# A delta-rule attention with a feed-forward part on one core: pieces placed by a time in us, a third place for converted weights, all low parts on TensorE

## The chip, the cores and the metric

One NeuronCore of a Trainium2 chip. The metric is the device time of one execution in microseconds (us). The core has five engines with a queue each: TensorE (PE; its weight loads are shown as PEld), VectorE (DVE), ScalarE (ACT), GpSimd (POOL) and SyncE (SP), which here only issues DMAs. An engine runs its instructions in the order in which they were written down for it; waits are semaphores.

## What is computed

```python
# q, k, v: (4, 8, 768, 48); beta: (4, 8, 768); w_in: (384, 2048); w_out: (2048, 384)
k_n = k / (norm(k) + 1e-6)
for t in range(S):                                   # per batch and head
    y[t] = q[t] @ state                              # state: 48 x 48
    state = state + beta[t] * outer(k_n[t], v[t] - state.T @ k_n[t])
x = y, heads side by side                            # (3072, 384)
h = x @ w_in
out = (h * tanh(softplus(h))) @ w_out                # (3072, 384)
```

The two weight matrices come as float64 numbers. The kernel reads them as pairs of 32-bit integers and makes of each number a high and a low part.

## The kernel before

**Chunks and units.** The sequence is cut into 12 chunks (`NS`) of 64 steps, for all 32 heads together. Chunk n gives 256 rows of x, and `moe(n)` runs the feed-forward part on them: this is unit n. A unit has eight pieces `fp`; `g1(fp)` is 18 matmuls of `h` (L528) and behind them a chain `e` over ScalarE and VectorE (L532 to L550) that ends in `g`, high and low part; `g2(fp)` is 12 matmuls into `acc` (L562), two pieces later. The low part of `g` is made by GpSimd in units 0 to 2 (`pg=3`) and by VectorE afterwards.

**Chunks, two at a time.** `early(g)` makes for chunks 2g and 2g+1 the products of the keys (`pg`), scales them (`ss`, `y`, `rc`, `nb`) and inverts a triangular matrix step by step on VectorE (`pr`, `gt`, L294 and L299), ending in transposes (`tt`, `tu`, `tn`). For g = 0 and 1 the inverse is made in two halves (28 steps), and `merge(n)` joins them with two matmul stages (`ma`, `mb`). Then come, per chunk, the stages `s_a`, `s_b` (`ta`, `tb`), and per half of the heads `s_gq`, `s_z`, `s_y` (`gq`, `pz`, `py` and `ps`), each followed by copies out of PSUM. `turn(n)` transposes the 256 rows `yy` (`xt`) and splits them into a high and a low `x`, with which unit n can start.

**Weights.** 28 pieces, 12 of `w_in` (names `ri`, `mi`, `wi`, 512 columns) and 16 of `w_out` (`ro`, `mo`, `wo`, 384 columns). `convert` (L177 to L204) turns one into a value `a` by one ScalarE and four VectorE operations, writes the high part rounded to float32r by ScalarE (L195), and for the first 22 pieces (`pl=22`) has TensorE add `a` and the high part through an identity in float32 (L199, L200; PSUM tile `lo`) and ScalarE write the low part (L201). The last six low parts are made by VectorE (L203). `a` has two places (tag `w`).

**The order.** `plan` holds generators with a time each, in units of a feed-forward pass from a table `TN`; they are advanced in the order of the times, and each writes down the whole of a piece at once, with the operations behind a matmul stage included. The instructions then go through a list scheduler that may move them on each engine within their dependencies and its own forecast of time. Two things bind it: `queue` chains instructions of VectorE in the written order (conversions, the first inverses, some of the stages of chunk 0), and from the time `m0=-0.05` on TensorE's order is as written. `keep_warm` writes filler matmuls on zeros behind chosen instructions (`warm`, L583).

Of the kernel before, what the change touches and what calls it, by code (L numbers as in the profile page):

```python
# [34 lines left out]
def kernel(  # L35
# [32 lines left out]
    P = 128  # L68
# [22 lines left out]
    nc.scalar.preload_act_table_set("natural_log_exp_and_others")  # L91

# [69 lines left out]
    chain = []  # L162

    def queue(ins, on=True):

        if not on:
            return
        if chain:
            order(ins, chain[-1])
        chain.append(ins)  # L170

# [4 lines left out]

    def convert(kind, i):  # L177
        st = raw[kind, i].rearrange("p (a b) -> p a b", b=2)
# [6 lines left out]
        nc.scalar.activation(a, high.bitcast(F32), AF.Abs, scale=2.0 ** -80)  # L185
        queue(nc.vector.tensor_scalar(a, a, F64_LEAST * 2.0 ** -80, F64_MOST * 2.0 ** -80, op0=ALU.max, op1=ALU.min))
        yield
        queue(nc.vector.tensor_scalar(ai, ai, 3, None, op0=ALU.logical_shift_left))
        yield
        queue(nc.vector.scalar_tensor_tensor(ai, high, 0x7FFFFFFF, ai, op0=ALU.bitwise_or, op1=ALU.bitwise_and))  # L190
        yield
        queue(nc.vector.scalar_tensor_tensor(ai, st[:, :, 0], 29, ai, op0=ALU.logical_shift_right, op1=ALU.bitwise_or))
# [3 lines left out]
        if parts.index((kind, i)) < TN['pl']:  # L196

            ps = pa.tile([P, 512], F32, tag="at", name=f"lo{kind}{i}")[:, :n]
            nc.tensor.matmul(ps, ident, a, start=True, stop=False)  # L199
            nc.tensor.matmul(ps, ident, w[:, 0].bitcast(F32), start=False, stop=True)  # L200
            nc.scalar.mul(out=w[:, 1], in_=ps, mul=-1.0)  # L201
        else:
            queue(nc.vector.scalar_tensor_tensor(w[:, 1], a, -1.0, w[:, 0], op0=ALU.mult, op1=ALU.subtract))  # L203
        yield  # L204
# [4 lines left out]
    def early(g):  # L209
# [3 lines left out]
        for t2 in range(2):  # L213
# [7 lines left out]
            queue(m, g < QK and g < 2)  # L221
            if g > 1:
                if TN.get('kp', 1):
                    tc.keep_in_program_order(m)
# [4 lines left out]
            for h8 in range(2):  # L229
                ps = pa.tile([P, 8, C], F32, tag="at", name=f"pg{n}_{h8}")  # L230
                for p8 in range(8):
                    p = 8 * h8 + p8

                    for c in range(2):
                        for hh in range(2):
# [22 lines left out]
        queue(nc.vector.tensor_scalar(ss, gf[:, ::33], 1e-30, None, op0=ALU.max), qg)  # L258
# [18 lines left out]
        queue(nc.vector.tensor_tensor(  # L277
            out=blk, in0=blk, in1=nb.rearrange("p (x j) -> p x j", x=nb_).unsqueeze(2).broadcast_to(by_col),
            op=ALU.mult), qg)
        nc.gpsimd.memset(gf[:, ::33], 1.0)  # L280
        bp = ap.tile([P, 32], F32, tag="bp", name=f"bp{g}")
        queue(nc.vector.tensor_scalar(bp, nb, -1.0, None, op0=ALU.mult), qg)
        ne = nes[g] = ap.tile([P, 32], F32, tag="ne", name=f"ne{g}")
        queue(nc.vector.transpose(ne, ss), qg)  # L284
        yield
        for j in range(1, sz - 1):
# [5 lines left out]
            eng = nc.gpsimd if g in TN.get('ps', ()) and TN.get('j0', 0) <= j < TN.get('j1', 31) else nc.vector  # L292
            on = qg and eng is nc.vector
            queue(eng.tensor_tensor(out=pv, in0=nj, in1=xj, op=ALU.mult), on)  # L294
            if g == 0 and j == TN.get('jt', 7):
                x = nc.tensor.matmul(warm[:, :64], zero[:, 0:P], pr[:, 0:64], start=True, stop=True)  # L296
                keep_warm(4 * TN.get('wt', 24), x)
            yield
            queue(eng.tensor_tensor(out=below, in0=below, in1=pv, op=ALU.add), on)  # L299
            yield  # L300
        queue(nc.vector.tensor_tensor(
            out=blk, in0=blk, in1=bp.rearrange("p (x i) -> p x i", x=nb_).unsqueeze(3).broadcast_to(by_col),
            op=ALU.mult), qg)
        if not split:
            yield
        queue(nc.vector.transpose(tt2[:, :, :, 32:].rearrange("p a b i -> p i (a b)"), gt), qg)
        tn = tns[g] = ap.tile([P, 2, NP, 32], F32, tag="tn", name=f"tn{g}", bufs=1)
        if split:
            tu = tus[g] = ap.tile([P, 2, NP, 16], F32, tag="prod", name=f"tu{g}", bufs=1)
            queue(nc.vector.transpose(tu.rearrange("p a b j -> p j (a b)"),  # L310
                                      gt[:, :, 0:16].rearrange("p i j -> p j i")), qg)
            ym = yms[g] = ap.tile([P, 33, 32], F32, tag="gt", name=f"ym{g}", bufs=1)
            nc.gpsimd.memset(ym[:, :32, 16:], 0.0)
        else:
            queue(nc.vector.transpose(tn.rearrange("p a b j -> p j (a b)"), gt.rearrange("p i j -> p j i")), qg)
# [9 lines left out]
    def merge(n):  # L325
# [3 lines left out]
        for h8 in range(2):  # L329
            pr = slice(8 * h8, 8 * h8 + 8)  # L330
            ps = pa.tile([P, 8, 16], F32, tag="at", name=f"ma{n}_{h8}")
            for p in range(8 * h8, 8 * h8 + 8):
                for qd in range(4):
                    r = slice(32 * qd, 32 * qd + 16)
                    m = nc.tensor.matmul(ps[32 * qd:32 * qd + 32, p % 8, :], dt[r, t2, p, :], tu[r, t2, p, :],
                                         start=True, stop=True)
            if g == 0:
                keep_warm(TN.get('wmg', 1), m)
            nc.scalar.mul(out=ym[:, pr, 0:16], in_=ps, mul=-1.0)
            yield  # L340
        for h8 in range(2):
            pr = slice(8 * h8, 8 * h8 + 8)
# [442 lines left out]
```

## Time and profile before

| | |
|---|---|
| median of 3 runs | 728.19 us (726.77 to 730.47) |
| profiled execution: time, span | 727.98 us, 726.0 us |
| mean granted clock of TensorE | 0.954 |
| TensorE busy | 649.3 us, 89% |
| VectorE busy | 488.0 us, 67% |
| ScalarE busy | 438.8 us, 60% |
| GpSimd busy | 81.9 us, 11% |
| HBM read, written | 31.56 MB, 4.72 MB |

The span is that of the one profiled execution, from the first to the last instruction; its time is 2 us longer. Busy time is the time in which an engine had an instruction under way; a share over the whole span mixes the head of the kernel (loads, first inverse, conversions) with the twelve units, so the head and the units have to be read apart.

### The profile page before, as it was taken

The numbers are of one execution on the slowest core, as the hardware profiler recorded it, in microseconds if no ns is written. First come the engines' busy times: TensorE is split into PE (matmuls) and PEld (weight loads), VectorE is DVE, ScalarE is ACT, GpSimd is POOL, SyncE is SP. The second block draws the span as 40 slices with busy tenths as digits, with TensorE's granted clock in tenths as the row PEclk, the third lists the DMA queues.
The fourth block names the chain that finished last, engine by engine and source line by source line (L and its number), as shares of the span: only waits on it lengthen the run. The fifth ranks groups of instructions, "written<-read, shape, count | busy, mean of one in ns | idle before, by whom it ended". The sixth has DMA issues, their size and how long they took to land.

```text
span 726.0 us, 23400 instructions
## 1 busy us (share of the span) xinstructions
PE 649.3 (89%) x10219; PEld 589.0 (81%) x10238; DVE 488.0 (67%) x1029; ACT 438.8 (60%) x815; POOL 81.9 (11%) x108
## 2 busy tenths in 40 slices
PE   6487888887899799997999998999969999999993
PEld 3144455677889799997999998999969999999993
DVE  4665586995349995479985699865898744543441
ACT  1123564764665557865667747577555787776771
POOL 5100001122222224100001010020100100000000
PEclk9696998997999999999999999999989999999998
DMA  5889140020152221331322312321111121000000
GB/s 86 212 236 339 28 63 7 3 34 15 14 86 42 41 38 42 46 57 23 45 57 36 56 24 45 56 38 27 40 23 30 37 36 34 13 15 10 8 16 22
DMA packets 160214, 37.79 MB, mean 52 GB/s; under 512 B 153456, under 2 KB 156528, under 8 KB 160112
## 3 DMA queue, kind: packets, MB, share of 16 engines
q1 hardware_dynamic: 160112, 36.30, 24.4%
q8 instruction: 80, 1.31, 0.7%
q14 instruction: 22, 0.18, 0.1%
HBM read 31.56 MB, written 4.72 MB: 50 GB/s over the span
## 4 chain that ended last, share of the span: by engine, by line
PE 58%; DVE 21%; ACT 7%; SPq 5%; issue 4%; DMA 3%; POOL 0%; DVEq 0%; ACTq 0%; POOLq 0%
PE h L528 21%; PE acc L562 19%; SPq L137 5%; DVE pr L294 3%; DVE gt L299 3%; PE gq L393 3%; DVE e L537 2%; PE py L393 2%; PE warm L583 2%; DVE xx L444 2%; DMA ri<-in_moe_w_in_dram 1%; DVE gt L250 1%; PE ta L393 1%; ACT e L534 1%; PE ps L393 1%
## 5 line engine op out<-in xcount | busy, mean ns | idle before, releaser
L528 PE MATMUL h<-x,wi 128*128 128x256 f32 x1728 | 229.2, 288 | 0.9 <-DVE e L537 0.9
L528 PEld LDWEIGHTS h<-x,wi 128*128 128x128 f32 x1728 | 221.9, 193 | 2.8 <-PE acc L562 0.9
L562 PE MATMUL acc<-wo,g 128*128 128x384 f32 x1152 | 223.0, 342 | 1.2 <-ACT e L534 1.1
L562 PEld LDWEIGHTS acc<-wo,g 128*128 128x128 f32 x1152 | 198.4, 188 | 5.6 <-ACT e L534 1.2
L537 DVE SCALAR_TENSOR_TENSOR e<-e,h 128x512 f32<-128x512 f32 x96 | 65.7, 685 | 89.1 <-ACT e L536 88.4
L534 ACT ACTIVATE e<-e 128x512 f32<-128x512 f32 x96 | 60.6, 631 | 68.5 <-DVE e L533 68.5
L532 ACT ACTIVATE e<-h 128x512 f32<-128x512 f32 x96 | 57.0, 594 | 53.3 <-PE h L528 49.3
L547 ACT CAST g<-e 128x512 fp32r<-128x512 f32 x96 | 59.3, 618 | 41.1 <-DVE e L537 40.3
L533 DVE TENSOR_SCALAR e<-e 128x512 f32<-128x512 f32 x96 | 43.8, 456 | 44.2 <-ACT e L532 43.8
L550 DVE TENSOR_TENSOR g<-e,g 128x512 fp32r<-128x512 f32 x72 | 49.9, 693 | 20.6 <-ACT g L547 19.0
L536 ACT ACTIVATE e<-e 128x512 f32<-128x512 f32 x96 | 60.6, 631 | 2.5
L535 ACT ACTIVATE e<-e 128x512 f32<-128x512 f32 x96 | 60.5, 630 | 2.4
L294 DVE TENSOR_TENSOR pr<-gt 128x84 f32<-128x84 f32 (+14 forms) x148 | 53.6, 362 | 4.8 <-PE warm L296 1.7
L299 DVE TENSOR_TENSOR gt<-gt,pr 128x84 f32<-128x84 f32 (+14 forms) x148 | 49.6, 335 | 3.1
L374 POOL TENSOR_TENSOR vt<-vt,ne 128x384 f32<-128x384 f32 x24 | 21.7, 904 | 219.1 <-DVE ne L284 94.6
L444 DVE TENSOR_TENSOR xx<-gq,amask 64x256 f32<-64x256 f32 x96 | 40.2, 418 | 6.3 <-PE gq L393 5.6
L550 POOL TENSOR_TENSOR g<-e,g 128x512 fp32r<-128x512 f32 x24 | 31.8, 1327 | 105.2 <-ACT g L547 70.5
L393 PE MATMUL gq<-xx,kt 64*64 64x112 f32 (+1 forms) x768 | 42.1, 256 | 0.8 <-ACT xx L484 0.7
L393 PE MATMUL py<-xx 128*64 128x48 f32 x768 | 41.3, 224 | 0.0
L393 PEld LDWEIGHTS py<-xx 128*64 128x64 f32 x768 | 37.6, 138 | 4.4 <-issue 1.5
L393 PEld LDWEIGHTS gq<-xx,kt 64*64 64x64 f32 x768 | 36.4, 133 | 4.9 <-issue 3.0
L393 PE MATMUL ps<-xx 128*48 128x48 f32 x704 | 37.4, 208 | 0.0
(102 smaller groups left out, 764.3 us busy)
## 6 DMA issues: line engine op xcount, KB each, us to landing
ri<-in_moe_w_in_dram SPq DMA_DIRECT2D x12, 512.0 KB
ro<-in_moe_w_out_dram SPq DMA_DIRECT2D x16, 384.0 KB
vt<-in_v_dram SPq DMA_DIRECT2D x48, 96.0 KB
xx<-in_k_dram SPq DMA_DIRECT2D x48, 96.0 KB
out_dram<-o SPq DMA_DIRECT2D x24, 192.0 KB
qsrc<-in_q_dram SPq DMA_DIRECT2D x48, 64.0 KB
ksrc<-in_k_dram SPq DMA_DIRECT2D x44, 64.0 KB
qsrc<-in_q_dram SPq DMA_DIRECT2D x48, 32.0 KB
```

The lines of the kernel that those rows point to most:

```text
L294: queue(eng.tensor_tensor(out=pv, in0=nj, in1=xj, op=ALU.mult), on)
L299: queue(eng.tensor_tensor(out=below, in0=below, in1=pv, op=ALU.add), on)
L393: last[:] = [nc.tensor.matmul(*a, start=True, stop=True)]
L528: nc.tensor.matmul(h[:, f2, :], wt["i", f * P // WI * NCH + c][:, i2, f0:f0 + P], x[:, c, :], start=(i == 0), stop=(i == 3 * NCH - 1))
L532: nc.scalar.activation(e, h, AF.Exp, scale=-1.0)
L534: nc.scalar.activation(e, e, AF.Square)
L535: nc.scalar.activation(e, e, AF.Ln, bias=0.5, scale=0.5)
L536: nc.scalar.activation(e, e, AF.Exp, scale=-1.0)
L537: nc.vector.scalar_tensor_tensor(e, e, -1.0, h, op0=ALU.add, op1=ALU.mult)
L547: nc.scalar.copy(out=gg[:, 0], in_=e)
L550: eng.tensor_tensor(out=gg[:, 1], in0=e, in1=gg[:, 0], op=ALU.subtract)
L562: nc.tensor.matmul(acc[t], gg[:, a, f2, ts_], wt["o", f][:, i2, :], start=(f == 0 and i == 0), stop=(f == NF - 1 and i == 2))
```

## The change

1. The plan is a heap of times in microseconds. `put(gen, *times)` sets one time for each step; `us(t)` turns a time in units into microseconds, with unit 0 at 76, unit 1 at 140, unit 2 at 192, unit 3 at 242 and 48 us for each later one. What follows a matmul stage (copies, masks, the chain `e`, the result's copies and stores) is put in by `defer` at a later time of its own, no longer at once.
2. VectorE is no longer chained (`queue` is gone). Up to 90 us nothing binds the scheduler, from 90 us TensorE's order is as written (`fixed`).
3. The converted value `a` has a third place: every third of the first 21 pieces uses `spare`.
4. All 28 low parts are made by TensorE; the high part goes through an identity in float32r, the value through the one in float32 as before. The PSUM tiles of the first eight come from the pool of `acc` (`po=8`).
5. The low part of `g` is made by VectorE in all units (`pg=()`).
6. 23 filler matmuls stand in the plan at 0.5, 16.5 and 18 us; those behind the stages are gone (73 records before).
7. Loads: one weight between the two loads of k, three before q, three before v. The stages have other times; scaling of v and transposing of q are pieces of their own, 5 and 4 us before their `s_gq`; for the second half the y copy is written before the copies of the state.

SyncE, start of the program, before: k of chunks 0 and 1 (the second into `qsrc`), one weight, beta, q, v.

```order
L137 DMA qsrc<-in_k_dram 32x16x32 x2
L137 DMA qsrc<-in_k_dram 32x16x16 x2
L137 DMA qsrc<-in_k_dram 32x16x32 x2
L137 DMA qsrc<-in_k_dram 32x16x16 x2
L137 DMA ri_146<-in_moe_w_in_dram 128x1024
L137 DMA betaT<-in_beta_dram 16x6x32 x8
L137 DMA qsrc<-in_q_dram 32x16x32 x2
L137 DMA qsrc<-in_q_dram 32x16x16 x2
L137 DMA qsrc<-in_q_dram 32x16x32 x2
L137 DMA qsrc<-in_q_dram 32x16x16 x2
L137 DMA vt_0_319<-in_v_dram 64x8x48 x2
L137 DMA vt_1_322<-in_v_dram 64x8x48 x2
```

And after, from the first weight on:

```order
L171 DMA ri_127<-in_moe_w_in_dram 128x1024
L171 DMA qsrc<-in_k_dram 32x16x32 x2
L171 DMA qsrc<-in_k_dram 32x16x16 x2
L171 DMA qsrc<-in_k_dram 32x16x32 x2
L171 DMA qsrc<-in_k_dram 32x16x16 x2
L171 DMA betaT<-in_beta_dram 16x6x32 x8
L171 DMA ri_145<-in_moe_w_in_dram 128x1024
L171 DMA ri_147<-in_moe_w_in_dram 128x1024
L171 DMA ro_149<-in_moe_w_out_dram 128x768
L171 DMA qsrc<-in_q_dram 32x16x32 x2
L171 DMA qsrc<-in_q_dram 32x16x16 x2
```

A weight now stands between the k loads and three more ahead of q.

VectorE, from the transposed key products to the first product of the inverse of chunks 0 and 1, before (`L258` is `ss`, `L294` the first product):

```order
L250 STREAM_TRANSPOSE gt_399<-d_156 128x1024
L258 TENSOR_SCALAR ss_403<-gt_399 128x32
L264 RECIPROCAL rc_408<-y_405 128x32
L265 SCALAR_TENSOR_TENSOR ss_403<-ss_403,rc_408 128x32
L266 SCALAR_TENSOR_TENSOR ss_403<-ss_403,y_405 128x32
L267 RECIPROCAL rc_408<-ss_403 128x32
L269 SCALAR_TENSOR_TENSOR nb_413<-rc_408 128x32
L270 TENSOR_TENSOR nb_413<-nb_413,betaT 128x32
L277 TENSOR_TENSOR gt_399<-gt_399,nb_413 128x2x16x16
L282 TENSOR_SCALAR bp_418<-nb_413 128x32
L284 STREAM_TRANSPOSE ne_420<-ss_403 128x32
L294 TENSOR_TENSOR pr_1_422<-gt_399 128x28
```

After (`L302` is `ss`, `L308` the reciprocal behind it; `L221` to `L227` are the four operations of a conversion on `mi`, `mo` or `spare`, `L421` the transposes of q):

```order
L225 SCALAR_TENSOR_TENSOR mi_245<-ri_145,mi_245 128x512
L221 TENSOR_SCALAR spare<-spare 128x512
L221 TENSOR_SCALAR mo_510<-mo_510 128x384
L302 TENSOR_SCALAR ss_418<-gt_414 128x32
L421 STREAM_TRANSPOSE xx_98<-qsrc 64x8x64
L227 SCALAR_TENSOR_TENSOR mi_245<-ri_145,mi_245 128x512
L421 STREAM_TRANSPOSE xx_99<-qsrc 64x8x64
L223 TENSOR_SCALAR spare<-spare 128x512
L223 TENSOR_SCALAR mo_510<-mo_510 128x384
L421 STREAM_TRANSPOSE xx_98<-qsrc 64x8x64
L421 STREAM_TRANSPOSE xx_99<-qsrc 64x8x64
L308 RECIPROCAL rc_430<-y_420 128x32
```

Operations on the second, third and fourth weight and the transposes of q now stand between rows that followed each other. Up to the transposes of the finished inverse (L306 before, L345 after) 4 conversions had their last VectorE operation on this queue before, 11 after; up to the first x of unit 0 it is 17 and 13.

ScalarE at the turn to unit 4, where `yy` is the copy of y that the transposes of the turn read; before:

```order
L534 ACTIVATE e_5_4718<-e_5_4718 128x512
L535 ACTIVATE e_5_4718<-e_5_4718 128x512
L536 ACTIVATE e_5_4718<-e_5_4718 128x512
L532 ACTIVATE e_6_4769<-h_6_4750 128x512
L547 CAST g_5_4725<-e_5_4718 128x512
L534 ACTIVATE e_6_4769<-e_6_4769 128x512
L535 ACTIVATE e_6_4769<-e_6_4769 128x512
L485 COPY yy_4370<-py_1_4781 128x384
L484 COPY xx_99<-ps_1_4782 48x8x48 x2
L536 ACTIVATE e_6_4769<-e_6_4769 128x512
L505 CAST x_4_4836<-xt_0_4838 128x3x128
```

And after:

```order
L588 ACTIVATE e_5_4660<-h_5_4641 128x512
L590 ACTIVATE e_5_4660<-e_5_4660 128x512
L591 ACTIVATE e_5_4660<-e_5_4660 128x512
L592 ACTIVATE e_5_4660<-e_5_4660 128x512
L525 COPY yy_4283<-py_1_4681 128x384
L522 COPY xx_99<-ps_1_4682 48x8x48 x2
L594 CAST g_5_4661<-e_5_4660 128x512
L588 ACTIVATE e_6_4750<-h_6_4731 128x512
L590 ACTIVATE e_6_4750<-e_6_4750 128x512
L591 ACTIVATE e_6_4750<-e_6_4750 128x512
L550 CAST x_4_4775<-xt_0_4777 128x3x128
```

The copy stood behind two operations of piece 6 and stands now ahead of all of them. On TensorE at that place the `py` and `ps` matmuls before the turn stood behind the `h` of piece 6 and stand now ahead of it. VectorE has there, ahead of the first operation on piece 5 (L533), 13 rows of the inverse without another one between; after, no more than 8 stand between two operations of the chain `e`.

The core of the diff:

```diff
-    TN = dict(c=[(-2.89,0),(-2.8,0),(-2,4),(-1.95,6),(-1.0,16),(-0.05,22),(0.35,28)],pl=22,...,pg=3,...,m0=-0.05)
+    TN = dict(fg=2, pl=range(0, 28), po=8, pg=(), db=1, fixed=((90.,()),(1e9,('PE',))),
+              d0=["k0",1,"k1","b",3,"q",3,"v","x",4,"k2",4,"k3",13],
+              us=[76., 140., 192., 242.],
+              warm=[(0.5,14),(16.5,3),(18.,6)],
...
+    def put(gen, *times):
+        for t in times:
+            heappush(plan, (t, next(count), gen))
...
+    def defer(wait, f, *a):
+        put(one(f, *a), now[0] + wait)
...
+    identr = mp.tile([P, NCH, UT], F32R, tag="x0", name="identr", bufs=2)[:, 0, 0:P]
+    spare = mp.tile([P, NCH * UT], F32, tag="x1", name="spare", bufs=2)[:, :512]
+    nc.vector.tensor_copy(identr, ident)
...
-        a = mp.tile([P, 512], F32, tag="w", name=f"m{kind}{i}")[:, :n]
+        if k % 3 < 2 or k >= 21:
+            a = mp.tile([P, 512], F32, tag="w", name=f"m{kind}{i}")[:, :n]
+        else:
+            a = spare[:, :n]
...
-            ps = pa.tile([P, 512], F32, tag="at", name=f"lo{kind}{i}")[:, :n]
+            if k < TN['po']:
+                ps = po.tile([P, 512], F32, tag=f"acc{k % 2}", name=f"lo{kind}{i}")[:, :n]
+            else:
+                ps = pa.tile([P, 512], F32, tag="at", name=f"lo{kind}{i}")[:, :n]
             nc.tensor.matmul(ps, ident, a, start=True, stop=False)
-            nc.tensor.matmul(ps, ident, w[:, 0].bitcast(F32), start=False, stop=True)
+            nc.tensor.matmul(ps, identr, w[:, 0], start=False, stop=True)
...
-            nc.scalar.activation(e, h, AF.Exp, scale=-1.0)
-            nc.vector.tensor_scalar(e, e, EXP20, 1.0, op0=ALU.min, op1=ALU.add)
...
-            eng = nc.gpsimd if n < TN.get('pg', 2) else nc.vector
+            eng = nc.gpsimd if n in TN['pg'] else nc.vector
+            t = 2.4
+            for d, f in ((0.7, lambda: nc.scalar.activation(e, h, AF.Exp, scale=-1.0)),
+                         (0.55, lambda: nc.vector.tensor_scalar(e, e, EXP20, 1.0, op0=ALU.min, op1=ALU.add)),
...
+                defer(t, f)
+                t += d
...
+            for f in (result, state) if h else (state, result):
+                f()
...
+    for until, engines in TN['fixed']:
+        if engines:
+            with tc.manual_schedule(engines={getattr(mybir.EngineType, e) for e in engines}):
+                run(until)
+        else:
+            run(until)
```

More of the change, by code (lines that the diff above doesn't have):

```diff
@@ L578, with keep_warm @@
     warm = ph.tile([P, 512], F32, tag="h", name="warm")
-    def keep_warm(n, after=None):
-        while n > 0:
-            m = nc.tensor.matmul(warm[:, :128 * min(n, 4)], zb[:, 0:P], zb[:, :128 * min(n, 4)], start=True, stop=True)
-            if after is not None:
-                order(m, after)
-            n -= 4
-    keep_warm(4 * TN.get('wm', 10))
+    def keep_warm(n):
+        tensor(0.4 * n)
+        for _ in range(n):
+            nc.tensor.matmul(warm, zb[:, 0:P], zb[:, :512], start=True, stop=True)
     ys, xs = {}, {}
@@ L672 @@
[L672 to L688 removed]
+    took = {s_a: 1.2, s_b: 1.2, s_gq: 1.1, s_z: 1.1, s_y: 1.9}
@@ new lines, in at @@
+    def at(t, *stages):
+        def run():
+            todo = [(f, a) for f, *a in stages if a[0] < NS]
+            tensor(sum(took[f] for f, _ in todo))
+            together(*(f(*a) for f, a in todo))
+        put(one(run), t)
+    for i, x in enumerate(TN['d0']):
+        put(one(loads, [x]), -1.0 if i < TN['d0'].index("q") else TN['e0'][3] + 0.1)
+    for t, n in TN['warm']:
+        put(one(keep_warm, n), t)
+    put(early(0), *TN['e0'], *spread(*TN['s0'], 28), TN['f0'])
+    put(merge(0), *TN['m0'])
@@ new lines @@
+    put(merge(1), *TN['m1'])
+    for h in range(2):
+        put(one(turn_q, 0, h), TN['tq'][h])
+        put(one(scale_v, 0, h), TN['sv'][h])
+        at(TN['gq0'][h], (s_gq, 0, h))
+    for t, st in zip(TN['st'], ((s_a, 0), (s_b, 0), (s_z, 0, 0), (s_z, 0, 1), (s_y, 0, 0), (s_y, 0, 1))):
+        at(t, st)
+    put(one(turn, 0), TN['x0'])
+    put(early(1), *TN['e1'], *spread(us(TN['s1'][0]), us(TN['s1'][1]), 28), us(TN['f1']))
+    put(merge(2), *map(us, TN['m2']))
+    put(merge(3), *map(us, TN['m3']))
@@ L690, with when @@
+    cuts = TN['cv']
+    def when(x):
+        for (t0, i0), (t1, i1) in zip(cuts, cuts[1:]):
+            if i0 <= x < i1:
+                return t0 + (t1 - t0) * (x - i0) / (i1 - i0)
+    for i, p in enumerate(parts):
+        ts = [when(i + j / 4 + 0.1) for j in range(4)]
+        end = ts[3] + 0.75
+        put(convert(*p), ts[0] - 0.75, *ts, end, end + 0.8, end + 1.4, end + 2.4)
     units = [moe(n) for n in range(NS)]
@@ new lines, with run @@
+        at(us(n - 2 + u[2]), (s_b, n + 1))
+    for g in range(2, NS // 2):
+        n = 2 * g
+        put(early(g), *(us(n + t) for t in (*(TN['g2'] if g == 2 else TN['gg']),
+                                            *spread(-2.6, TN['sg'], 30 if g < FG else 63), -1.43)))
+        if g < FG:
+            put(merge(n), *(us(n + t) for t in TN['mg']))
+            put(merge(n + 1), *(us(n + t + 0.12) for t in TN['mg']))
+    def run(until):
+        while plan and plan[0][0] < until:
+            now[0], _, gen = heappop(plan)
+            next(gen, None)
```

317 lines of the change are left out of this document (134 added, 183 removed).

## The prediction

> **What bounds the kernel now.** I read the windows first, cut where the units begin, then the waits of TensorE, then the order of time of each engine in the first 130 us. A unit is one of the twelve passes through the feed-forward part; the columns are the length of the stretch, the busy time of TensorE, weight loads, VectorE, ScalarE and GpSimd, the granted clock, the DMA share and GB/s.
>
> ```profile
> span 726.0 us, 23400 instructions
> 0.00:47.50 47.50, 30.54 (x335) 14.32 (x340) 25.27 (x70) 10.17 (x19) 11.97 (x29) 0.86 0.75 165
> 47.50:105.00 57.50, 45.44 (x830) 27.44 (x842) 39.90 (x76) 28.90 (x57) 3.41 (x5) 0.85 0.54 161
> 105.00:198.30 93.30, 76.25 (x1904) 64.55 (x1896) 66.20 (x149) 51.40 (x103) 17.56 (x20) 0.91 0.11 18
> 198.30:299.10 100.80, 95.09 (x1531) 91.04 (x1520) 73.33 (x148) 62.47 (x118) 27.89 (x27) 0.98 0.32 52
> 299.10:593.00 293.90, 279.84 (x4422) 271.80 (x4421) 227.97 (x489) 198.36 (x367) 21.09 (x28) 0.98 0.23 40
> 593.00:726.00 133.00, 122.10 (x1238) 119.88 (x1236) 55.29 (x100) 87.44 (x155) 0.00 (x0) 0.98 0.06 16
> ```
>
> From 198.3 us on TensorE is busy 497.0 of 527.7 us: there it is the bound and only its idle gaps can be won. Before that, 198.3 us pass for work that keeps TensorE busy 152 us and VectorE 131 us. The matmuls of h (L528) show where the units lie: 144 of them are one unit, and the second unit's begin only at 198.3.
>
> ```profile
> 105.00:198.30 93.30, 21.11 (x144) 19.31 (x144) 0.91 0.11 18
> 198.30:251.50 53.20, 20.31 (x144) 19.34 (x145) 0.97 0.37 59
> ...
> 123.16 2.49 PE L528 MATMUL h<-x,wi 128*128 128x256 f32 x17
> ```
>
> One h matmul was at 105, the other 17 of its group at 123.16. So the head of the kernel is a chain (inverse on VectorE, merge, stages, turn), and behind it conversions of weights. Two places in it are plain losses: VectorE stood 6.33 us because the converted value's two places were full (ScalarE's L185 waited for a low part, and that stood behind the block of filler matmuls on TensorE), and TensorE ran those fillers for 8.64 us and more.
>
> ```profile
> 44.46 0.36 DVE L186 TENSOR_SCALAR mo<-mo 128x384 f32<-128x384 f32 x1 [6.33 <-ACT mo L185]
> 47.50 1.93 DVE L306 STREAM_TRANSPOSE tt<-gt 128x1024 f32<-128x1024 f32 x1
> 31.70 8.64 PE L583 MATMUL warm<-zero 128*128 128x512 bf16 x34
> ```
>
> **Head of the kernel up to the inverse.** The times in the table of stages do not hold in the first 90 us, because no engine is fixed there: the order of VectorE shows 11 conversions whose four VectorE operations stand ahead of the transposes of the finished inverse (L345, L349), where before there were 4. Three of the 7 more have 512 columns, four 384.
>
> ```profile
> L190 DVE SCALAR_TENSOR_TENSOR mi<-ri,mi 128x512 int32<-128x512 int32 x12 | 8.2, 684 | 0.2
> L192 DVE SCALAR_TENSOR_TENSOR mi<-ri,mi 128x512 int32<-128x512 int32 x12 | 8.2, 683 | 0.2
> L188 DVE TENSOR_SCALAR mi<-mi 128x512 int32<-128x512 int32 x12 | 5.1, 424 | 0.2
> L186 DVE TENSOR_SCALAR mi<-mi 128x512 f32<-128x512 f32 x12 | 5.0, 418 | 4.4 <-ACT mi L185 4.4
> L381 DVE STREAM_TRANSPOSE xx<-qsrc 64x512 f32<-64x512 f32 x48 | 33.9, 706 | 3.2 <-PE ps L393 1.6 <-PE py L393 0.2
> ```
>
> A 512-wide one is 2.21 us; at between three quarters of that and all of it for the others, the 7 cost 13 to 15.5 us, I take 14. Four transposes of q (2.8 us) and one of k (about 1.2, a little under two of L381) come ahead too. VectorE's 25.3 us before L306 become 25.3 + 14 + 2.8 + 1.2 = 43.3 us. When can they be done? The row that starts the chain proper (ss) now stands behind the first operation on the second, third and fourth weight, so it waits for DMA. SyncE's issues:
>
> ```profile
> 0.80 4.11 SPq L137 DMA_DIRECT2D ksrc<-in_k_dram  x8
> 9.21 0.49 SPq L137 DMA_DIRECT2D ri<-in_moe_w_in_dram  x1
> 9.74 5.96 SPq L137 DMA_DIRECT2D betaT<-in_beta_dram  x8
> 15.82 5.23 SPq L137 DMA_DIRECT2D qsrc<-in_q_dram  x8
> 23.84 1.09 SPq L137 DMA_DIRECT2D ri<-in_moe_w_in_dram  x2
> 28.28 0.66 ACT L185 ACTIVATE mi<-ri 128x512 f32<-128x512 f32 x1 [8.67 <-DMA ri<-in_moe_w_in_dram]
> ```
>
> In the new order k, one weight, k, beta come to 0.8 + 4.1 + 0.5 + 4.1 + 6.0 = 15.5 us; the next three weights are issued by 17. From issue to use took 28.28 - 24.4 = 3.9 us (the first of the two at 23.84). So weight 2 is there at about 20, weight 4 at 21 to 23, ss runs at about 24, and the transposes of q behind it (issued 17 to 22, landing 2 to 4 us later) end near 28. Of the 43.3 us some 13.5 lie ahead of ss (9.3 us of the first 20 us before, plus two conversions). Taking 26 as the point from which VectorE is never idle, the inverse's first transpose starts at 26 + 30 = 56 and the second ends at 59. Before: 47.5 and 50. **The inverse comes 9 us later, not earlier.** Bounds: 53 (no DMA wait beyond the k loads) and 75 (every one of the weights 2 to 8 waited for as the row at 28.28 was).
>
> **From the inverse to the first h.** Before, 47.5 to 123 us, with 39.9 us of VectorE's work in 57.5. Now 13 conversions are done by then, against 17, and only 16 us of VectorE's rows stand between the inverse and the turn, most of them dependent on the chain itself. What is left is seven TensorE stages, copies between them and three low parts.
>
> ```profile
> 289.57 1.20 PE L393 MATMUL ta<-tt,at 32*32 32x32 f32 x64
> 64.35 1.92 PE L393 MATMUL ta<-tt,at 32*32 32x32 f32 x64 [0.47 <-issue]
> 83.65 1.14 PE L393 MATMUL pz<-vt,tt 64*64 64x48 f32 x32
> L406 ACT ACTIVATE at<-ta 32x512 f32<-32x512 f32 x24 | 14.0, 585 | 7.3 <-PE ta L393 6.9
> L422 ACT COPY tt<-tb 32x512 f32<-32x512 f32 x24 | 13.7, 572 | 0.6 <-PE tb L393 0.3
> L485 ACT COPY yy<-py 128x384 f32<-128x384 f32 x24 | 11.1, 462 | 0.4 <-PE ps L393 0.4
> 42.77 1.02 PE L199 MATMUL loi<-mi,ident 128*128 128x512 f32 x2
> ```
>
> Seven stages of 1.2 to 2 us (11), copies of 0.5 to 1.2 (8), three low parts of about 1 us (3): 22 us. A low part costs 2 x 1.02 us now; with the float32r identity the second half is one pass, which an estimate from the h matmuls below (2.13/18 us for 256 columns) puts at 0.24. Clock: 73 fillers become 23, all in front of the first pg by TensorE's order, so they end near 10 us and nothing fills the gaps afterwards. The two rows of ta (1.92 us at 64, 1.20 at 290, where the granted clock was 0.98 on average) give a factor of 1.6 on some 14 us of TensorE, 8 us if all of it is slow; I take half, 4. First h at 59 + 26 = 85, the low half of x at 86. Bounds: 81, and 123 as before.
>
> **Unit 0.** VectorE carries it: 15 conversions remain instead of 11 (+8 us by 2.0 each), eight low parts of g come from GpSimd (+5.5), six low parts of weights go to TensorE (at most -4), and rows that GpSimd stretched become short again.
>
> ```profile
> L550 DVE TENSOR_TENSOR g<-e,g 128x512 fp32r<-128x512 f32 x72 | 49.9, 693 | 20.6 <-ACT g L547 19.0
> L294 DVE TENSOR_TENSOR pr<-gt 128x88 f32<-128x88 f32 x4 | 3.6, 888 | 0.0
> L294 DVE TENSOR_TENSOR pr<-gt 128x108 f32<-128x108 f32 x12 | 3.2, 269 | 2.0 <-PE warm L296 1.7
> ...
> 120.00:140.00 20.00, 16.14 (x275) 11.93 (x264) 19.64 (x48) 11.97 (x25) 4.49 (x6) 1.00 0.01 2
> 140.00:160.00 20.00, 18.49 (x275) 16.88 (x274) 19.75 (x53) 15.38 (x29) 3.44 (x3) 1.00 0.22 31
> ...
> 272.97 2.11 PE acc L562 x12
> 275.10 2.37 PE h L528 x18
> 281.47 2.13 PE h L528 x18
> ```
>
> The 88-wide product took 888 ns, more than three times the wider 108-wide one, beside GpSimd's part of g. So 66.2 + 8 + 5.5 - 4 - 4 (such rows) - 1 (the transpose of k already done) = 71 us, and VectorE ran at 98% when it was full. TensorE has 8 x 2.13 of h, 6 x 2.11 of acc, 15 low parts and the stages, about 63 us at full clock, under that cover; if the cover were gone it would set 63. I add 3 for waits: unit 1 begins at 86 + 74 = 160 instead of 198.3, **-38.3**. Bounds 148 and 180.
>
> **Units 1 and 2.** Two grams, the merge of chunks 2 and 3 and three stages moved out of unit 0 into unit 1: eight pieces of about 1.1 us (by ta's 1.20), +9 on TensorE, against 5.7 us of idle time in 198.3 to 299.1. VectorE gets 16 low parts of g, 11 us, into 27 us of idle time. Between +3 and +14, I take **+6**.
>
> **Units 3 to 8.** TensorE's idle time is one wait:
>
> ```profile
> PE xt L503 <- ACT yy L485: 13.2, 3, 6.2
> ```
>
> The y copy stands on ScalarE behind e's operations, and these behind 13 rows of the inverse on VectorE at the turn to unit 4. Now the y stage is one h group (2.13 us) further ahead of the turn, the copy stands ahead of the last group's e, and at most 8 such rows separate two e rows there. I take two thirds: **-9**, between 0 and -14. The last three units, 133 us, stand as they are; TensorE is full there up to the drain.
>
> **Sum.** 726.0 - 38.3 + 6 - 9 = 684.7 us of span. The profiled execution took 727.98 for its span of 726.0, 0.2 under the median of 728.19, so I add 2: 687 us.
>
> **Rivals.**
> 1. Packed: VectorE's work alone decides. With 8 us of idle time before 48 us of work the inverse ends at 54, the first h is at 77, unit 1 at 148, units 1 and 2 take +3, and the whole wait of 13.2 goes: 726 - 50 + 3 - 13 + 2 = 668. For it: VectorE reached 98% at 120 to 160. Against: the DMA waits above.
> 2. Late: the weights ahead of ss land late, DMA being 0.75 busy in the head. The inverse ends at 75, everything behind it is 16 us later: 703. For it: the 8.67 us that ScalarE waited for ri. Unit 0 has fewer conversions to wait for then, which speaks against the full price.
> 3. Slower, the clock: no filler stands after 10 us, TensorE works in short pieces, and the clock stays at half through the stages and all of unit 0. The stages cost 4 us more (first h at 90), and unit 0's 63 us of TensorE at the factor of 1.6 to 2 become 100 to 126, unit 1 begins at 203: 726 + 5 + 6 - 9 + 2 = 730. It decides from a unit 0 that begins the next unit after 201 us. Against: at 120 to 160 the clock was 1.00 with TensorE busy 16 to 18 of 20 us between conversions, and no filler ran then.
> The Trainium skill, "TensorE: Matmul & The Clock Gate", Part 1, speaks for this rival: there the half rate is the default, full rate comes after about 3.4 us of sustained work and goes after an idle window of that length. By it fillers at the very front buy nothing for a stage at 60 us; the trace agrees as far as ta at 64.35 was slow, with a filler block only 22 us before.
> 4. The stage times come true after all (unit 1 at 140, unit 3 at 242): 726 - 57 - 9 + 2 = 662. Against it stands VectorE's order itself: 43 us of work cannot end by 34.5.
>
> **How the numbers follow.** The forecast (676 to 696) has 0.50, packed and the plan come true (660 to 676) 0.20, late (696 to 718) 0.19, the clock and others that end near or above 724 0.11, of which 0.02 within 0.5%. A measurement of this kernel tells about 0.5% from no change. The range leaves out half of the slow cases and the lowest: 660 to 714.
>
> **What would show it.** Right: L345 near 56, xt of unit 0 near 83, h of unit 1 near 160, VectorE over 90% busy in between, the wait of xt for yy under 5 us in units 3 to 8. Wrong in the head: L345 under 50 or over 70, or ss without a DMA wait ahead of it. Wrong by the clock: the granted clock below 0.8 in unit 0. Wrong in units 1 and 2: a length outside 104 to 115 us.

## The result, and the profile after

The changed kernel took 703.29 us (median of 4 runs, 702.13 to 704.33) against 728.54 of the kernel before in the same session (726.77 to 730.47): a ratio of 0.9652, with a 95% interval of 0.9623 to 0.9682. That is 25 us faster, inside the range of 660 to 714 and 16 us slower than the 687 forecast. The profiled execution took 702.13 us for a span of 700.3.

The stretches of the span of after, cut where its units begin (columns as in the prediction):

```profile
0.00:47.50 47.50, 27.65 (x303) 13.63 (x303) 33.73 (x78) 17.47 (x34) 12.07 (x29) 0.78 0.77 177
47.50:98.80 51.30, 32.58 (x917) 27.59 (x918) 25.15 (x59) 14.74 (x32) 4.59 (x7) 0.57 0.57 165
98.80:170.30 71.50, 64.84 (x1131) 54.69 (x1131) 63.42 (x153) 53.72 (x109) 3.97 (x6) 1.00 0.20 31
170.30:236.70 66.40, 58.58 (x1356) 54.79 (x1344) 44.45 (x104) 34.75 (x67) 5.89 (x9) 0.95 0.26 42
236.70:284.00 47.30, 47.21 (x822) 45.31 (x823) 34.01 (x70) 33.18 (x61) 4.17 (x6) 1.00 0.26 44
284.00:566.40 282.40, 279.98 (x4423) 267.08 (x4422) 222.22 (x489) 195.90 (x364) 18.06 (x27) 1.00 0.24 41
566.40:700.30 133.90, 122.77 (x1237) 119.43 (x1235) 55.46 (x100) 90.19 (x158) 0.00 (x0) 0.97 0.06 16
```

Set against the rows of before: unit 1 begins at 170.4 instead of 198.4 (-28.0), units 1 and 2 take 113.7 instead of 100.8 (+12.9), units 3 to 8 take 282.3 instead of 293.9 (-11.6), the last three 133.9 instead of 133.0 (+0.9). The sum is -25.8, and the spans differ by 25.7.

The head ran nearly as forecast (ss at 26.14, the inverse's first transpose at 55.68, predicted 24 to 26 and 56). What did not is the stretch from there to the first h: 40 us instead of 26. TensorE and VectorE in order of time, and three windows of that stretch:

```profile
57.45 0.99 DVE L349 STREAM_TRANSPOSE tu<-gt 128x512 f32<-128x512 f32 x1
58.58 1.90 PE L375 MATMUL ma<-tu,d 16*32 16x16 f32 x128 [13.51 <-DVE tu L349]
65.45 1.36 PE L386 MATMUL mb<-tt,ym 32*32 32x16 f32 x83 [4.33 <-issue]
71.64 1.59 PE L433 MATMUL ta<-tt,at 32*32 32x32 f32 x51 [2.43 <-issue]
83.90 2.08 PE L238 MATMUL loi<-spare,ident 128*128 128x512 f32 x2
86.59 0.36 DVE L221 TENSOR_SCALAR spare<-spare 128x384 f32<-128x384 f32 x1 [9.23 <-ACT spare L219]
98.84 0.39 PE L575 MATMUL h<-x,wi 128*128 128x256 f32 x2
```

```profile
61.00:65.40 4.40, 0.12 (x8) 0.01 (x2) 0.00 (x0) 0.00 (x0) 0.00 (x0) 0.50 1.03 416
69.20:71.70 2.50, 0.07 (x4) 0.06 (x4) 0.43 (x2) 0.00 (x0) 0.00 (x0) 0.50 0.57 74
80.00:90.00 10.00, 10.00 (x315) 8.24 (x313) 3.03 (x7) 4.00 (x9) 0.83 (x2) 0.50 0.01 3
```

Three things are to be seen. The granted clock is half without a break (48.3 to 92.7 us in the clock's records), even from 80 to 90, where TensorE is never idle. Twice TensorE stands for "issue", 6.8 us in all: it waits for no other instruction, the first time while the DMA engines are full (1.03). And VectorE converts nothing from 51 to 86 us: all three places of the converted value hold a value whose low part is still to come, and the first of these low parts, that of spare, stands on TensorE behind the stages, at 83.9. Each of the three got a theory: A, the clock; B, program code that comes late; C, the stalled conversions.

The profile's view of the DMA queues bears on B. In the window of each gap it has one packet on a queue that it marks "instruction", of 16 KB (61.00 to 65.40, then 69.20 to 71.70):

```profile
q8 instruction: 1, 0.02, 1.4%
```

```profile
q8 instruction: 1, 0.02, 2.6%
```

The first packet ended at 63.98 and the second at 70.35; TensorE went on at 65.45 and 71.64, 1.5 and 1.3 us later.

### The profile page after: what moved, and what is told of

Its sections match the earlier page's. It is cut to its first block, busy times and chain, and to the rows that moved or that the text cites. A ratio compares the mean times of both kernels' runs of the same rounds, so it can differ in the third digit from the quotient of the medians.

```text
span 700.3 us, 23223 instructions
## 1 busy us (share of the span) xinstructions
PE 633.6 (90%) x10163; PEld 582.5 (83%) x10163; DVE 478.4 (68%) x1048; ACT 440.0 (63%) x821; POOL 48.8 (7%) x84
## 4 chain that ended last, share of the span: by engine, by line
PE 44%; DVE 26%; ACT 13%; SPq 7%; issue 6%; DMA 3%; DVEq 0%; ACTq 0%
PE h L575 15%; PE acc L610 15%; SPq L171 7%; DVE e L593 4%; PE gq L433 3%; ACT e L591 3%; DVE g L595 3%; DVE pr L336 3%; DVE gt L338 3%; ACT e L590 2%; PE py L433 2%; ACT e L592 2%; DVE e L589 2%; DVE xx L480 2%; DVE xx L421 2%
## 5 line engine op out<-in xcount | busy, mean ns | idle before, releaser
L575 PEld LDWEIGHTS h<-x,wi 128*128 128x128 f32 x1728 | 214.4, 188 | 10.5 <-DVE e L593 2.9
L610 PEld LDWEIGHTS acc<-wo,g 128*128 128x128 f32 x1152 | 198.4, 188 | 3.2
L594 ACT CAST g<-e 128x512 fp32r<-128x512 f32 x96 | 59.5, 619 | 41.3 <-DVE e L593 40.8
L595 DVE TENSOR_TENSOR g<-e,g 128x512 fp32r<-128x512 f32 x96 | 65.1, 678 | 20.6 <-ACT g L594 19.4
L589 DVE TENSOR_SCALAR e<-e 128x512 f32<-128x512 f32 x96 | 40.8, 425 | 25.1 <-ACT e L588 24.8
L338 DVE TENSOR_TENSOR gt<-gt,pr 128x84 f32<-128x84 f32 (+14 forms) x148 | 46.0, 311 | 3.2
L336 DVE TENSOR_TENSOR pr<-gt 128x84 f32<-128x84 f32 (+14 forms) x148 | 45.9, 310 | 2.5
L433 PE MATMUL gq<-xx,kt 64*64 64x112 f32 (+1 forms) x768 | 44.6, 264 | 0.9 <-ACT wo L243 0.9
L433 PE MATMUL pz<-vt,tt 64*64 64x48 f32 x768 | 38.0, 235 | 2.4 <-ACT tt L462 1.3
L433 PEld LDWEIGHTS pz<-vt,tt 64*64 64x64 f32 x768 | 34.4, 139 | 6.3 <-ACT tt L462 2.8
```

The source lines that it names most:

```text
L336: nc.vector.tensor_tensor(out=pv, in0=nj, in1=xj, op=ALU.mult)
L338: nc.vector.tensor_tensor(out=below, in0=below, in1=pv, op=ALU.add)
L433: last[:] = [nc.tensor.matmul(*a, start=True, stop=True)]
L575: nc.tensor.matmul(h[:, f2, :], wt["i", f * P // WI * NCH + c][:, i2, f0:f0 + P], x[:, c, :], start=(i == 0), stop=(i == 3 * NCH - 1))
L594: (0.7, lambda: nc.scalar.copy(out=gg[:, 0], in_=e)),
L595: (0.8, lambda: eng.tensor_tensor(out=gg[:, 1], in0=e, in1=gg[:, 0], op=ALU.subtract))):
```

## The experiments

All are made from the changed kernel; runs 3, 5, 6 and 8 hold run 2's edit as well. The diffs are cut to the lines that matter. A ratio is that to the kernel before, which ran again beside each run; the changed kernel did not, so a run is set against its 703.29 us and 0.9652. "Orders held" means that extra edges keep TensorE, VectorE and ScalarE in the order they have in the changed kernel.

**1. Fillers up to the merge (A).**

```diff
+    TN = dict(fill=[(55.5,52,7,512)], ...
...
+    def fill(n, k, width=512):
+        for _ in range(n):
+            nc.tensor.matmul(warm[:, :width], identr, wt[parts[k]][:, 0, :width], start=True, stop=True)
...
+    for t, n, k, width in TN['fill']:
+        put(one(fill, n, k, width), t)
```

> 52 extra matmuls (identity times an already converted weight, 512 columns) stand on TensorE between the last low part at 44 us and the first merge matmul at 58.6; nothing else moves. Theory A (the half clock made the chain long): the records of the changed kernel show the clock at half from 59.5 to 103.9 us and TensorE busy some 32 us from 58.6 to 98.8; with the clock up at 58.6 the merge's 128 matmuls take about 1.1 instead of 1.90 us, the first h comes at 88 to 91 instead of 98.8 and the kernel takes about 694. Theory B (TensorE waits for its own program code): the gaps of 4.33 us at 65.5 and 2.43 us at 71.6 stay, the clock falls back in the first of them, the first h comes at 96 to 98 and the kernel takes 700 to 703.

Measured: 713.19 us, ratio 0.9792 (0.9757 to 0.9827), 10 us slower than without. (The clock's times in the expectation are counted from the start of the records; from the span's start they are 48.3 to 92.7.) The fillers in order of time:

```profile
45.17 13.76 PE L638 MATMUL warm<-wi,identr 128*128 128x512 f32 x52
```

Two windows behind them, and units 0 and 1:

```profile
60.00:65.00 5.00, 3.22 (x249) 3.18 (x250) 0.82 (x2) 0.56 (x2) 0.52 (x1) 0.62 1.02 397
65.00:70.00 5.00, 1.67 (x33) 1.63 (x34) 1.27 (x3) 0.00 (x0) 0.90 (x2) 0.50 1.03 413
...
99.10:178.00 78.90, 67.93 (x1132) 56.94 (x1130) 65.38 (x153) 54.31 (x110) 3.91 (x7) 0.95 0.20 30
178.00:248.40 70.40, 61.88 (x1341) 58.11 (x1335) 45.32 (x103) 33.85 (x66) 5.51 (x9) 0.91 0.23 36
```

The clock was full to 61.2 us and fell there, 0.5 us into the merge's small matmuls and after 1.5 us in which TensorE waited for the inverse; the first h came at 99.1. The gap marked issue was still there, 4.42 us. Of the extra 15 us of span 12.8 lie in units 0 to 2 (78.9, 70.4 and 48.8 us against 71.6, 66.4 and 47.3), where no filler stands. What changed there is order: no engine but TensorE is fixed, and with the fillers emitted the scheduler chose another order, for VectorE from 129 us on, in the rows ahead of the second inverse. Run 5 tests that.

**2. The last 13 weights loaded late (B).** One small GpSimd write into each of their tiles, ordered behind the second merge's copies, holds their loads back to about 90 us; a scaling of v on GpSimd is ordered behind the same copies.

```diff
-              d0=[... "k2",4,"k3",13],
+              d0=[... "k2",4,"k3"],
...
+            if gate:
+                order(nc.gpsimd.memset(r.bitcast(F32)[:, 0:1], 0.0), gate[-1])
...
+    put(one(loads, [13]), 63.0)
```

> The loads of the last 13 weights wait until the second merge is done (about 90 us) instead of running until 72 us; the order of TensorE, VectorE and ScalarE is unchanged. Theory B (the two gaps marked issue at 65.5 and 71.6, 6.8 us in all, are program code that comes through DMA engines which the weights keep full, share 1.03 from 58 to 69 us): both gaps fall below 1 us, the first h comes at 91 to 93, the kernel takes 695 to 698. Theory A (clock alone): the gaps may go, but the stages stay at half rate, and with 15th and later weights landing at 91 to 104 us unit 0 loses nothing. If the gaps stay, they are not the DMA's doing and the time stays at 703. Bad case: conversions wait for weights at 103 us and later and unit 0 grows by 3 to 5 us.

Measured: 699.04 us, ratio 0.9604 (0.9568 to 0.9641). The remaining gap in order of time:

```profile
64.38 1.36 PE L389 MATMUL mb<-tt,ym 32*32 32x16 f32 x83 [1.59 <-issue]
```

Its window, and the stretch from the merge to the first h:

```profile
62.80:64.40 1.60, 0.02 (x4) 0.02 (x3) 0.00 (x0) 0.00 (x0) 0.00 (x0) 0.50 0.00 0
...
60.20:94.00 33.80, 30.37 (x917) 25.73 (x918) 14.86 (x31) 12.87 (x29) 5.05 (x20) 0.65 0.24 74
```

The second gap is gone, the first shrank from 4.33 to 1.59 us and stays there with the DMA engines idle. One of 0.90 us came at 85.5, which run 12, the same kernel, has not. So 4 to 5 of the 6.8 us were the doing of these 13 loads. Here the first packet marked instruction behind the merge's start ended at 62.81, 2.6 us after the first matmul of the merge, and in the changed kernel 5.4 us after it; TensorE went on 1.6 and 1.5 us behind the packet. Merge to first h fell from 40.3 to 33.8 us with the same order on all three engines, and unit 0 took 71.3. B holds, a little under its price.

**3. Both edits.**

> Both edits of the two runs before. If A and B are both true and independent, the stages run at full clock from 58.6 on without the two gaps: inverse to first h in 24 to 28 us, the first h at 83 to 86, the kernel at 684 to 688, which is the forecast on record. If only one holds, the time is that of the better of the two runs alone. Rival C (VectorE's conversions stand still from 50 to 86 us, so that an earlier h only meets more of them): unit 0 grows from 71.6 us by as much as the chain shrinks.

Measured: 710.52 us, ratio 0.9768 (0.9722 to 0.9813). Merge to first h took 34.0 us, as in run 2 alone, and units 0 and 1 were nearly as long as in run 1 (77.5 and 69.5). The clock fell at 60.8 us, ahead of the merge's first matmul at 61.13, in 3.4 us of TensorE's waiting for the inverse. As A was put, it falls: these fillers did not carry the clock into the stages. Fillers without a pause up to the merge were not tried.

**4. Conversions that go on (C).**

```diff
-po=8
+po=20
+        if k >= 11:
+            order(m, inverse[0])    # m: VectorE's first operation, L221
```

> The low parts of the first 20 weights take their place in the two accumulator banks instead of the banks that the stages share (whose places are given out in the order of emission), and the conversions from the 12th on stand on VectorE behind the inverse's last transpose. Theory C (the conversions stood still from 50 to 86 us since their low parts stood behind the stages): VectorE works 10 to 14 us more between 58 and 99 us, about 19 conversions instead of 13 are done before the low half of x, and unit 0 shrinks from 71.6 to 60 to 63 us, where TensorE is full; the chain itself grows by 0 to 4 us for the low parts that now stand between its stages; the kernel takes 692 to 696. Theory A or B alone: the chain's 40 us and unit 0's 71.6 us stay within 3 us in sum, the kernel takes 700 to 705.

Measured: 703.40 us, ratio 0.9666 (0.9638 to 0.9694), no change. Merge to first h, and unit 0:

```profile
61.40:105.40 44.00, 32.61 (x984) 27.35 (x985) 25.67 (x52) 17.72 (x38) 5.30 (x7) 0.68 0.42 117
105.40:172.00 66.60, 60.38 (x1056) 53.13 (x1054) 54.69 (x131) 46.90 (x94) 3.71 (x6) 0.95 0.21 33
```

The conversions went on as meant: VectorE worked 25.7 us from merge to first h instead of 14.9, and unit 0 lost 8.7 us of VectorE and 5.0 of length. But merge to first h grew by 3.7. It was not the low parts' time on TensorE, which was busy 32.6 us there in both kernels (here with more matmuls at a higher clock). It waited once for ScalarE:

```profile
91.25 1.90 PE L389 MATMUL mb<-tt,ym 32*32 32x16 f32 x128 [3.79 <-ACT ym L380]
```

That copy of the second merge stands on ScalarE behind an operation of a conversion and four copies of pz; VectorE's and ScalarE's orders were free here and changed. The stall of VectorE is real, but as it was filled here, the chain paid for what unit 0 gained. The same with the copies first was not tried.

**5. Fillers among the stages, orders held, weights late.** 50 fillers ahead of the merge and then one behind about every 32 small matmuls.

> The kernel with the last 13 weights loaded late (699.0 us, inverse to first h 33.8 us from the merge on), the order of TensorE, VectorE and ScalarE held to that of the changed kernel, and fillers put into TensorE's order by hand: 50 between the last low part and the first merge matmul, and then about one 512-column filler behind every 32 small matmuls of the merges and stages (31 in all, 6.6 us at 0.213). Theory A2 (matmuls of 16 to 64 rows and columns do not raise the clock however densely they come, but a few full-width matmuls between them do): the clock is full through the stages, 128 merge matmuls take 1.2 to 1.4 instead of 1.9 us, the first h comes 24 to 27 us after the first merge matmul, and the kernel takes 690 to 693. Rival (one in 32 is too few): the clock stays at half, the fillers cost 0.43 us each and the kernel takes 703 to 706. Theory O (the 10 us that the first filler kernel lost came from VectorE's other order in units 0 and 1, not from the fillers): units 0 and 1 keep 71.3 and 66.3 us within 1 us here.

Measured: 698.68 us, ratio 0.9585 (0.956 to 0.9611), the time of run 2. Its windows from the merge to the first h:

```profile
60.70:70.30 9.60, 9.13 (x295) 6.23 (x295) 2.11 (x5) 0.55 (x2) 1.71 (x3) 0.50 0.29 49
70.30:80.00 9.70, 9.70 (x264) 6.88 (x263) 3.80 (x8) 3.27 (x6) 0.00 (x0) 1.00 0.02 4
80.00:90.00 10.00, 9.75 (x308) 6.08 (x308) 4.21 (x9) 4.19 (x10) 3.32 (x17) 1.00 0.17 40
90.00:96.80 6.80, 6.64 (x83) 4.61 (x82) 4.74 (x11) 4.85 (x12) 0.00 (x0) 1.00 1.02 396
```

Half of the stage tb in order of time, and behind it the whole stage in run 2:

```profile
74.08 0.69 PE L438 MATMUL tb<-at,tn 32*32 32x32 f32 x32
```

```profile
71.31 1.92 PE L438 MATMUL tb<-at,tn 32*32 32x32 f32 x64
```

The sparse fillers did raise the clock: full from 70.3 us on, 32 matmuls of tb in 0.69 us instead of half of 1.92. From the first ta to the first h it took 26.3 us, against 26.5 in run 2: TensorE is busy nearly all the time, so 22 fillers of 0.2 to 0.3 us there used up what the clock gave. By that the half clock costs an estimated 5 to 7 us in that part, and this way of buying it costs as much. Units 0 and 1 kept 71.6 and 66.1 us with 79 more fillers in the kernel (29 among the stages, not 31 as expected): the loss of run 1 was the other order, not the fillers.

**6. k of chunk 5 loaded ahead of q and v of chunk 3, weights late.**

```diff
-us(TN['prep2'] if n == 2 else n - 1.85)
+us(TN['prep2'] if n == 2 else 1.27 if n == 3 else n - 1.85)
```

> The kernel with the last 13 weights loaded late (699.0), and the q and v loads of chunk 3 issued behind the k loads of chunk 5 instead of ahead of them; no other queue changes its order. Theory Q (unit 1 is 66 us long since SyncE's queue stands 19 us at v loads that wait for a free buffer, so that k arrives late, VectorE's transpose and the gram matmuls wait 3.4 us and the clock falls back for 7 us): unit 1 takes 60 to 63 us, the kernel 694 to 696. Rival (unit 1 is long for its eleven more pieces of work on TensorE): 65 to 66 us, the kernel 698 to 700.

Measured: 700.93 us, ratio 0.9626 (0.9608 to 0.9645). TensorE's and VectorE's waits in 165 to 237 us, in run 2 and then here:

```profile
PE pg L285 <- DVE kt L266: 2.2, 1, 2.2
...
DVE kt L266 <- DMA ksrc<-in_k_dram: 1.0, 1, 1.0
```

```profile
PE pg L285 <- DVE kt L266: 2.1, 1, 2.1
...
DVE kt L266 <- DMA ksrc<-in_k_dram: 0.9, 1, 0.9
```

Against run 2, from which it is made, the edit hardly touched the wait, so it is no test of Q, and unit 1 took 67.9 us instead of 66.3. What speaks against Q is run 2 itself: in the changed kernel the two waits were 3.4 and 2.2 us, and unit 1 was as long there (66.4). What keeps TensorE idle for 8 us of unit 1 stays open.

**7. The old stage times in units 3 and later.**

```diff
-cc=(0.05,0.28,0.5,0.72)
+cc=(0.05,0.3,0.55,0.8)
```

> The changed kernel with the four times of the stages of units 3 and later set back (0.05, 0.3, 0.55, 0.8 instead of 0.05, 0.28, 0.5, 0.72 of a unit). Theory (the y stage one h group earlier is what took away the 13.2 us that the transposes of xt waited for yy): that wait comes back with 8 to 14 us, units 3 to 8 take 290 to 296 instead of 282.3, the kernel 711 to 717. Rival (the wait went with the shorter runs of the inverse's rows on VectorE and ScalarE's order, not with the times): 282 to 285 us and 703 to 705.

Measured: 709.26 us, ratio 0.9741 (0.9715 to 0.9767). TensorE's longest sum of waits in 284 to 575 us:

```profile
PE xt L548 <- ACT yy L525: 7.5, 3, 2.6
```

The wait is back, three times as before, and units 3 to 8 took 289.4 us (284.4 to 573.8). So the times, with the orders of VectorE and ScalarE that follow from them from unit 3 on, carry 7.1 of the 11.6 us; the other 4.5 were not undone by this edit.

**8. Runs 2, 4 and 6 together.**

> Three edits together: the last 13 weights late, the conversions from the 12th on behind the inverse with their low parts in the accumulator banks, the k loads of chunk 5 first. If the gaps of TensorE's program code go as in the late-weights run (5.5 us of such gaps stood in the run with conversions alone) and unit 1 loses 4 us: 692 to 695. If the order that VectorE gets in unit 0 costs as much as it did in the first filler run: 702 to 708. If unit 1's length is not SyncE's doing: 696 to 699.

Measured: 703.49 us, ratio 0.9663 (0.9645 to 0.9682). First h at 99.1, unit 0 71.3 us, unit 1 67.6. The gain of run 2 is not there: unit 0, whose order the scheduler had changed once more, was no shorter than in the changed kernel, and unit 1 was 1.2 us longer.

**9. The float32 identity again, orders held.**

```diff
-            nc.tensor.matmul(ps, identr, w[:, 0], start=False, stop=True)
+            nc.tensor.matmul(ps, ident, w[:, 0].bitcast(F32), start=False, stop=True)
```

> The changed kernel with the order of TensorE, VectorE and ScalarE held as it is, and the second half of each of the 28 low parts multiplied with the float32 identity again. By the rows of before (1.72 us for a 512-column low part at full clock, against 1.19 us now) a low part costs 0.5 us more at full clock and up to 1 us more at half. Theory (TensorE carries the chain from inverse to first h, VectorE unit 0): the five low parts in the chain add 3 to 5 us ahead of the first h, the fifteen in unit 0 nothing more than 2 us; the kernel takes 706 to 710. Rival (low parts lie in waits everywhere): 703 to 705.

Measured: 714.34 us, ratio 0.9823 (0.9797 to 0.9848), 11 us slower. Unit 0:

```profile
103.50:180.40 76.90, 72.86 (x1149) 57.72 (x1147) 63.66 (x152) 54.37 (x109) 5.17 (x8) 0.98 0.20 31
```

The chain grew by 2.5 us (merge to h 42.7), unit 0 by 5.3, units 1 and 2 by 3.4. In unit 0 VectorE has the same 63.7 us of work, TensorE 72.9 instead of 64.8: with 8 us more of TensorE's work the unit is 5.3 us longer. Both theories were too low.

**10. Without the 23 front fillers, orders held** (`warm=[]`).

> The changed kernel with the orders held and without its 23 fillers at the front of TensorE's order. Theory (they end near 10 us; the clock of the chain, half from 48.3 to 92.7 us, does not depend on them): the first gram's 64 matmuls of 32 columns are at half rate, the inverse comes 0 to 1 us later, the kernel takes 702 to 705. Rival (the gram ahead of ss is on the chain of work): the inverse comes 2 to 3 us later and the kernel takes 705 to 707.

Measured: 702.42 us, ratio 0.9663 (0.963 to 0.9695): they buy nothing. ss came at 26.8, the inverse's first transpose at 58.3, as in most other runs here (57.4 to 59.1; run 7's 55.9 and the changed kernel's 55.68 are the early ones).

**11. g's low parts of units 0 to 2 on GpSimd, orders held** (`pg=(0,1,2)`).

> The changed kernel with the orders held and the low parts of g of units 0, 1 and 2 (24 of them) on GpSimd instead of VectorE. Theory (VectorE carries unit 0): it loses 5.5 us there, but rows beside GpSimd's part stretch by some 4 us, as before, so unit 0 takes 70 to 73 us; units 1 and 2, where VectorE waits 20 us and more, keep 113 to 114 us; the kernel takes 702 to 705. Rival (GpSimd's slower part delays acc and the e chain): units 0 and 1 grow by 3 to 8 us, the kernel takes 706 to 714.

Measured: 709.77 us, ratio 0.9759 (0.9735 to 0.9782), 6.5 us slower. The inverse's 14 additions (L338) that fall into unit 0, as windows of that line alone (length, VectorE's busy time, clock, DMA share, GB/s), in the changed kernel and then here:

```profile
98.50:170.30 71.80, 3.34 (x14) 1.00 0.21 31
```

```profile
98.50:170.30 71.80, 5.56 (x14) 0.98 0.18 27
```

GpSimd's group of g's low parts here (busy, mean ns, its idle time before):

```profile
L595 POOL TENSOR_TENSOR g<-e,g 128x512 fp32r<-128x512 f32 x24 | 31.3, 1303 | 123.1 <-ACT g L594 95.4 <-issue 27.7
```

A low part takes 1303 ns on GpSimd and 678 on VectorE, and rows of VectorE stretch beside it; VectorE's busy time from 98.5 to 170 is 63.2 us, not 5.5 less than 63.4. Unit 0 took 74.5 us, unit 1 68.3, units 2 and 3 2.5 more.

**12. Run 2 again, in five rounds.**

> The kernel with the last 13 weights loaded late once more, in more rounds: 697 to 700 us, a ratio to the kernel before of 0.957 to 0.963, that is 0.4 to 0.8% less than the changed kernel. If its gain in the first look was the accident of that chip: 702 to 704.

Measured: 699.19 us, ratio 0.9605 (0.9583 to 0.9628), merge to first h 33.3 us. It beats both kernels, by 4 us or 0.5% the changed one: the two intervals just touch, but its runs (697.0 to 699.4 us) and those of the changed kernel (702.1 to 704.3) do not overlap. Run 5 equals it.

## Why the prediction was right in sign and where it was off

The span is 15.6 us over the 684.7 of the sum: 13.8 up to the first h (98.8 instead of 85), -3.4 in unit 0, +6.9 in units 1 and 2, -2.6 in units 3 to 8 and +0.9 in the last three.

- **Head up to the inverse: right.** +9 us was priced from conversions ahead of the inverse and the wait for weights; the profile has +8.2, run 7 +8.4 and the others +10 to +12. VectorE's work up to there was 41.3 us, 43.3 priced. The wait ahead of ss was more TensorE's than the weights', though: VectorE stood 4.51 us for the second chunk's key products, which the prediction did not name, and 1.34 us for the second weight's conversion.
- **Inverse to first h: the step that failed, 26 us priced, 40.3 measured** from the first merge matmul. The sum had 18 us of TensorE ("seven TensorE stages" 11, three low parts 3, the clock 4), 8 of copies and nothing else. TensorE was busy 32.6 us there: its order holds the second chunk's merge and five low parts ahead of h as well, and all but the last 6 us ran at half clock, where half of the price was taken. No term held the 6.8 us of gaps marked issue; loading 13 weights later gave 4 to 5 of them back. The profile of before had such a row (3.37 us at 63.58, merge matmuls), left unpriced. The copies erred the other way: other than for issue TensorE stood idle only 0.9 us, since copies of one stage run beside matmuls of another. 32.6 + 6.8 + 0.9 is 40.3.
- **Unit 0: right in size, by luck.** 71.6 us against 74. The sum had 71 us of VectorE's work and 3 of waits; measured are 63.4 and 8.1, two misses that cancel. "VectorE carries it" is not shown either: TensorE was busy 64.8 of these 71.6 us, a little more than VectorE, so there was hardly a cover, and run 9 shows that 8 us more of its work made the unit 5.3 us longer. The float32r identity, priced at nothing in unit 0 for that cover, is worth 11 us of the whole. The low parts of g were priced at +5.5 less 4 there; run 11 shows no cost in VectorE's busy time, and 6.5 us gained in the whole kernel.
- **Units 1 and 2: +12.9 against +6** (bounds 3 to 14). The moved pieces were priced well (TensorE 105.8 busy instead of 95.1, +10.7 for +9), but I let idle time absorb 3 us, and idle grew from 5.7 to 7.9 us.
- **Units 3 to 8: right**, -11.6 against -9. The wait of 13.2 us is gone, and run 7 brings 7.5 of it back by setting back the stage times.
- **Rivals.** "The clock stays at half" was half true: through the stages, as its condition says, but not in unit 0 (1.00), where h's matmuls run. What the Trainium skill says ("TensorE: Matmul & The Clock Gate", Part 1: full rate after about 3.4 us of sustained work) is not enough here: from 71.6 to 92.7 us TensorE had one gap, of 0.72 us, and stayed at half. "Late" gave 703 us, which is what was measured, but that is luck: the inverse was not late, and the weights' loads cost 4 to 5 us behind it, in TensorE's gaps.
- **Signs named in advance.** L345 came at 55.68 (near 56), xt of unit 0 at 96.06 (near 83), h of unit 1 at 170.4 (near 160), with VectorE 89% busy in unit 0 (over 90%); the wait of xt for yy is gone from units 3 to 8.

Not settled: how much of the 4.5 us left in units 3 to 8 belongs to which edit, and the idle time of unit 1. The third place was not taken away alone, and VectorE's chaining (`queue`), the new order of the loads and the later times of what follows a stage were not undone by themselves.

## What to carry to other kernels

Price a stretch from the queue: count every row that stands on the engine between its two ends, by the order, with the duration of the clock it will run at, and not the stages that the stretch is named after. An engine that is to cover another at 89% leaves 10%: write down what the second engine's work comes to, since a few microseconds turn the bound round. And where the scheduler is free, an edit that adds anything moves the order elsewhere: hold the order before believing a difference of a per cent or two.

## What the hardware showed that was not expected

- TensorE's granted clock does not follow from how busy it is alone. From 80 to 90 us it was busy 10.00 of 10 us at 0.50, with small matmuls (ma, pz, mb, then py and ps of 48 columns) and one low part. In run 5, with a 512-column filler of full height behind about every 32 such matmuls, 1.00 came at 70.3 us, 9.6 us after the merge began; in run 2, without fillers, it came at 83.9. What in the filler does it (its columns, its rows, its type, which was bf16) no run separates.
- TensorE waited 4.33 and 2.43 us for no other instruction where the DMA engines were busy (share 1.03 and 0.57); with 13 weights loaded later, 1.59 us and none. In the 14 profiles TensorE has 50 gaps of over 0.7 us marked issue, and each of them ends 1.2 to 1.6 us after a 16 KB packet marked instruction ended, also where the DMA engines were idle. So these gaps look like waits for program code. That the packet is TensorE's own code rests on this timing: no row names the engine.
